# A transformer block on one core: the MLP gate computed on VectorE during fc1, `rows` of three vectors, and the last store issued without other stores' waits

## The chip, the cores and the metric

The kernel runs on one core of a Trainium2 chip. A core has a matrix engine (TensorE, "PE" in the profile; its weight loads are listed as "PEld"), a vector engine (VectorE, "DVE"), a scalar engine (ScalarE, "ACT"), a general engine (GpSimd, "POOL"), a sync engine that issues most transfers (SyncE, "SP"), and 16 DMA engines that all queues share. Operands lie in SBUF, an on-chip memory of 128 partitions; matmul results lie in PSUM, eight banks of 512 f32 values per partition. The engines run their own instruction lists and wait for one another by semaphores. The metric is the device time of one execution in microseconds (us), smaller is better.

## The reference

One block of a diffusion transformer, two samples of 256 tokens, width D = 1152, two heads, MLP width 4608, all in bf16:

```python
mod = (_silu(c) @ w_mod).reshape(B, 6, 1, D)
shift_a, scale_a, gate_a, shift_m, scale_m, gate_m = [mod[:, i] for i in range(6)]
h = _layernorm(x) * (1 + scale_a) + shift_a
q, k, v = split(h @ wqkv)
a = attention(q, k, v) @ wo
x = x + gate_a * a
h2 = _layernorm(x) * (1 + scale_m) + shift_m
m = _gelu(h2 @ w_fc1) @ w_fc2
return x + gate_m * m
```

The condition `c` has one row per sample; each of the six modulation vectors has 1152 values per sample. The change concerns how the last one, `gate_m` (the "MLP gate"), is computed. Its only use is the product with the result of fc2, at the very end.

## The kernel before, in words

All of SBUF is one tensor, `arena`, and all of PSUM one tensor, `psum`; every buffer is a slice at a fixed offset, and several buffers share an offset one after another. Therefore the profile names only `arena` and `psum`, and steps are told apart by source lines.

The program is recorded as units of work, each with an engine, a modelled duration and its reads and writes. `Sched.schedule` orders the units: TensorE's and SP's lists stay in the order of the source, the other engines take the ready unit with the longest modelled path behind it. `Sched.emit` turns dependences into semaphore waits. TensorE's records all carry line 681 (matmul) or 684 (transposition), those of transfers line 662.

The stages in TensorE's order, with the names used later:

1. `silu(c)` becomes a 128x18 tile `ST` (nine chunks of 128 values for two samples). The scale vectors of the attention, the normalization of `x`, then the projections of K and Q; `sh`, the shift vector, by `quad_mm`: four matmuls at a time, each of two rows (the samples) on its own 32-partition quadrant of the array (line 895 transposes its result).
2. Scores, softmax, the value projection `v_proj`, and between two of its parts `rows`.
3. `pv` (probabilities times values), the output projection `wo_tile` with the gated residual (line 1034 multiplies by the attention gate `GA` on VectorE, line 1035 adds `x` on POOL), the second normalization, and `xn2_T`, which transposes on TensorE and applies scale and shift of the MLP on VectorE (1053) and ScalarE (1056) into `H2T`.
4. fc1: 36 tiles of 128 MLP columns. The first eight run for 256 tokens at a time, the others for 512; ScalarE applies Gelu (1066) and writes `GT[f]`.
5. fc2: for each of four token tiles three pieces of 384 columns (the last piece of the last tile is cut into 224, 96 and 64 columns after its first 384-column pieces). VectorE multiplies by the MLP gate `GM` (1145) and adds the residual (1146), SP stores.

`rows` multiplies `ST` by `WMODR`, four of the six column blocks of `w_mod`: attention gate, MLP shift, MLP scale, MLP gate. For each of nine contraction chunks it fills three PSUM banks with four quadrants of 384 columns each, 108 matmuls. ScalarE copies the two gates to `ROWS` (676), VectorE transposes shift and scale into per-partition form (976). POOL then issues four small stores of the gates to a scratch tensor in DRAM and four loads that broadcast them to all 128 partitions (`GA`, and `gate_load(1, GM)` for the MLP gate).

SP issues the transfers strictly in order, and a wait of one holds up those behind it. Behind the weights of attention come `ld_modr` (`WMODR`), `ld_wo`, the first four fc1 weight blocks, three quarters of the fc2 weights `WFC2`, its last quarter, the other five fc1 blocks, and the output stores. `WFC2` lies on the place that `WMODR` has before. Ahead of the last store, SP waits until all stores but the last two have landed (lines 469 to 471); at the end of the program it waits for the last two (485, 486).

Of the kernel before, what the change touches and what calls it, by code (L numbers as in the profile page):

```python
# [171 lines left out]
class Sched:  # L172
# [225 lines left out]
    def emit(self, nc, block, sems, dma_sems):  # L398
        order = self.order
        eidx = {e: 0 for e in ENGINES}  # L400
        dma_cnt = [0] * len(dma_sems)
        n_other = getattr(self, "n_other_dma_sems", 8)
        n_sp = len(dma_sems) - n_other
        di = 0
        dj = 0
        for e in ENGINES:
            for u in order[e]:
                for ins in u.instrs:
                    if u.dma_bytes > 0:
                        if e == "sp":  # L410
                            k = di % n_sp
                            di += 1
                        else:
                            k = n_sp + dj % n_other
                            dj += 1
                        dma_cnt[k] += 16
                        ins.dma_sem = k
                        ins.dma_val = dma_cnt[k]
                    else:
                        eidx[e] += 1  # L420
                        ins.eidx = eidx[e]
        self.final_counts = dict(eidx)
        self.final_dma = list(dma_cnt)
        snap = {}
        stats = {"waits": 0}

        def sem_of(d):
            if d.dma_sem is not None:
                return ("d", d.dma_sem), d.dma_val
            return ("e", d.unit.eng), d.eidx  # L430

        allu = sorted(self.units, key=lambda u: (u.start, u.uid))
        known = {e: {} for e in ENGINES}
        waits = {}
        for u in allu:
            e = u.eng
            kn = known[e]
            for ins in u.instrs:
                need = {}
                for d in ins.deps:  # L440
                    k, v = sem_of(d)
                    if need.get(k, 0) < v:
                        need[k] = v
                wl = []
                for k, v in sorted(need.items(), key=lambda kv: (-kv[1], str(kv[0]))):
                    if kn.get(k, 0) >= v:
                        continue
                    wl.append((k, v))
                    kn[k] = v
                    for d in ins.deps:  # L450
                        if sem_of(d) == (k, v):
                            sn = snap.get(d.gidx)
                            if sn:
                                for kk, vv in sn.items():
                                    if kn.get(kk, 0) < vv:
                                        kn[kk] = vv
                            break
                waits[ins.gidx] = wl
                stats["waits"] += len(wl)
                snap[ins.gidx] = dict(kn)  # L460
        self.wait_stats = stats

        outs = [ins for u in order["sp"] for ins in u.instrs if ins.is_out]
        last_out = outs[-1]

        def run_engine(e, eng_handle):
            for u in order[e]:
                for ins in u.instrs:
                    if ins is last_out:
                        for o in outs[:-2]:  # L470
                            eng_handle.wait_ge(dma_sems[o.dma_sem], o.dma_val)
                    for (k, v) in waits[ins.gidx]:
                        if k[0] == "d":
                            eng_handle.wait_ge(dma_sems[k[1]], v)
                        else:
                            eng_handle.wait_ge(sems[k[1]], v)
                    bi = ins.fn(eng_handle)
                    if ins.dma_sem is not None:
                        bi.then_inc(dma_sems[ins.dma_sem], 16)
                    else:  # L480
                        bi.then_inc(sems[e], 1)
            if e == "sp":
                for o in outs[-2:-1]:
                    eng_handle.wait_ge(dma_sems[o.dma_sem], o.dma_val)
                eng_handle.wait_ge(dma_sems[last_out.dma_sem], last_out.dma_val)

        block.sync(lambda eng: run_engine("sp", eng))
        block.tensor(lambda eng: run_engine("pe", eng))
        block.scalar(lambda eng: run_engine("act", eng))
        block.vector(lambda eng: run_engine("dve", eng))  # L490
        block.gpsimd(lambda eng: run_engine("pool", eng))
# [4 lines left out]
F32 = mybir.dt.float32  # L496
ALU = mybir.AluOpType
# [47 lines left out]
def build_kernel(nc, x, c, wqkv, wo, w_mod, w_fc1, w_fc2, out):  # L545
# [5 lines left out]
    with (  # L551
# [44 lines left out]
        WO = wmat(O_B, D)  # L596
        WSH = wmat(O_C, D)
        WV = wmat(O_C, D)
        WMODR = wmat(O_R, 4 * D)
        WFC2 = sb(O_R, 4 * W1).rearrange("p (k f) -> p k f", k=JT)  # L600
        WFC1 = [wmat(o, 512) for o in (O_A, O_A + 9216, O_C, O_C + 9216)]
        X = sb(O_X, 9216).rearrange("p (t d) -> p t d", t=4)
# [11 lines left out]
        GA = [sb(O_GA + b * 2304, 2304) for b in range(2)]  # L614
        GM = [sb(o + 18432, 2304) for o in (O_A, O_C)]
        XN2 = [sb(O_R + 4 * W1 - (i + 1) * 2304, 2304) for i in range(4)]
        ROWS = sb(O_R + 4 * W1 - 5 * 2304, 2304)[:, 0:576].rearrange("p (g n) -> p g n", g=2)
        T1 = [sb(O_X + i * 1536, 1536, F32) for i in range(3)]
        OST = [sb(O_X + 4608 + i * 768, 768) for i in range(3)]
        gt_offs = ([O_P + i * 1024 for i in range(8)] + [O_B + i * 1024 for i in range(20)]  # L620
# [8 lines left out]
        HC = sb(misc(72), 72, F32)  # L629
        ST = sb(misc(36), 36)  # L630
        SHA = sb(misc(1152), 1152, F32)
        SC1A = sb(misc(72), 72, F32)
        MT = sb(misc(2304), 2304, F32)
        SHM = MT[:, 0:288]
# [82 lines left out]
        act(200, lambda e: e.activation(out=TH, in_=CT_PS, func=ACTF.Tanh, scale=0.5), [CT_PS], [TH], "c_tanh")  # L717
        dve(170, lambda e: e.tensor_scalar(out=HC, in0=CT_PS, scalar1=0.5, scalar2=None, op0=ALU.mult), [CT_PS], [HC], "c_half")
        dve(170, lambda e: e.scalar_tensor_tensor(out=ST, in0=TH, scalar=1.0, in1=HC, op0=ALU.add, op1=ALU.mult), [TH, HC], [ST], "c_silu")


        def ln_stats_dve(src, chunks, bn_t, mv_t, rstd_t, tag):
# [167 lines left out]
            quad_mm(0, WSH[:, kt, :], 0, 9, kt)  # L890
        dma(WV, wqkv_v[:, :, 2 * D:3 * D], D * D * 2, "ld_wv", run=2304)
        for k0 in range(0, KT, 3):
            dma(WMODR[:, k0:k0 + 3, :], wmod_v[:, k0:k0 + 3, 2 * D:6 * D], 3 * P * 4 * D * 2, "ld_modr%d" % k0)
        MT1 = ps32(0, 0, 288)
        dve(c_dve_psum32(288), lambda e: e.transpose(SHA, MT1), [MT1], [SHA], "sha")  # L895
        for kt in range(KT):
# [66 lines left out]
            copy_on("act" if v_rr[0] % 2 else "dve", V[:, t, ci * CH:(ci + 1) * CH], o, CH, False, "v_ev%d_%d" % (t, ci))  # L963


        row_banks = (3, 4, 5)

        def rows():
            S.unit("pe", KT * 3 * c_mm(CH) + 200.0, "rows")
            for kt in range(KT):  # L970
                for r in range(3):
                    quad_mm(row_banks[r], WMODR[:, kt, :], 12 * r, 12 * r + 12, kt)
            copy_on("act", ROWS[:, 0, :], ps32(3, 0, 288), 288, False, "rows_ev0")
            for i, (bank, c0, n, d0) in enumerate(((3, 288, 96, 0), (4, 0, 384, 96), (5, 0, 96, 480))):
                src, dst = ps32(bank, c0, n), MT[:, d0:d0 + n]
                dve(c_dve_psum32(n), lambda e, src=src, dst=dst: e.transpose(dst, src), [src], [dst], "mt_%d" % i)
            sc, so = MT[:, 288:576].rearrange("p (k r) -> p k r", r=32)[:, :, 0:2], SC1M.rearrange("p (k b) -> p k b", b=2)
            dve(170, lambda e: e.tensor_scalar(out=so, in0=sc, scalar1=1.0, scalar2=None, op0=ALU.add), [sc], [so], "sc1m")
            copy_on("act", ROWS[:, 1, :], ps32(5, 96, 288), 288, False, "rows_ev1")
            for gi in range(2):  # L980
                for b in range(2):
                    dma(scratch[gi, b].rearrange("(k q c) -> q k c", q=4, c=32), ROWS[b:128:32, gi, :].rearrange("p (k c) -> p k c", c=32),
                        2304, "st_g%d%d" % (gi, b), eng="pool")
                if gi == 0:
                    gate_load(0, GA)

        def gate_load(gi, G):
            for b in range(2):
                dma(G[b], scratch[gi, b].partition_broadcast(P), P * D * 2, "ld_g%d%d" % (gi, b), eng="pool")


        PVB = [(0, 1, 2, 6, 7), (3, 4, 5, 0, 1)]
# [29 lines left out]
        def wo_tile(t, before={}):  # L1022
# [16 lines left out]
            dve(170, lambda e: e.scalar_tensor_tensor(out=nm, in0=m, scalar=-1.0, in1=rs, op0=ALU.mult, op1=ALU.mult), [m, rs], [nm], "nmr2_%d" % t)  # L1039
            act(1344, lambda e: e.activation(out=xn2, in_=x1, func=ACTF.Identity, scale=rs, bias=nm), [x1, rs, nm], [xn2], "xn2_%d" % t)  # L1040

        def xn2_T(t):
            b = t // 2
            xn2 = XN2[t]
# [4 lines left out]
            for kt in range(KT):  # L1049
                o, dst = slot[kt], H2T[:, kt, t * 128:(t + 1) * 128]  # L1050
                s1, s2 = SC1M[:, kt * 2 + b:kt * 2 + b + 1], SHM[:, kt * 32 + b:kt * 32 + b + 1]
                if kt < (4 if t < 2 else 6):
                    dve(335, lambda e, o=o, dst=dst, s1=s1, s2=s2: e.tensor_scalar(out=dst, in0=o, scalar1=s1, scalar2=s2, op0=ALU.mult, op1=ALU.add),  # L1053
                        [o, s1, s2], [dst], "h2T_%d_%d" % (t, kt))
                else:
                    act(440, lambda e, o=o, dst=dst, s1=s1, s2=s2: e.activation(out=dst, in_=o, func=ACTF.Identity, scale=s1, bias=s2),  # L1056
# [42 lines left out]
        v_proj(3, 0)  # L1099
        v_proj(3, 1)  # L1100
        v_proj(3, 2)
        gate_load(1, GM)
        wfc1_load(2)
        wfc1_load(3)
        for q4 in range(3):
            dma(WFC2[:, 9 * q4:9 * q4 + 9, :], wfc2_v[:, 9 * q4:9 * q4 + 9, :], 9 * P * D * 2, "ld_wfc2_%d" % q4, run=2304)
        for b in range(2):
            for h in range(2):
# [12 lines left out]
        for f in range(F0 - 2, F0):  # L1121
            fc1_tile(f, 0, 256)
        dma(WFC2[:, 27:36, :], wfc2_v[:, 27:36, :], 9 * P * D * 2, "ld_wfc2_3", run=2304)
        for f in range(F0):
            fc1_tile(f, 256, 256)
        for f in range(F0, JT):
            if f % 4 == 0 and f // 4 >= 4:
                wfc1_load(f // 4)
            fc1_tile(f, 0, 512)

        oi = 0
        for t in range(4):
# [70 lines left out]
```

## Time and profile before

| | |
|---|---|
| median of three runs | 248.95 us (248.63 to 249.59) |
| the profiled execution | 249.1 us, span in the profile 247.1 us |
| granted TensorE clock, mean | 0.996 |
| TensorE (PE) busy | 240.4 us, 97% |
| VectorE (DVE) busy | 69.9 us, 28% |
| ScalarE (ACT) busy | 64.0 us, 26% |
| POOL busy | 21.1 us, 9% |
| DMA | 51.59 MB, 27708 packets |

The span is the profile's own window; the execution's time also holds what lies around it. The page gives busy shares per engine and in 40 slices of the span (each 6.18 us), the chain of work that ended last (followed back from the last instruction to what released it), and groups of instructions with the idle time ahead of them. In a timeline the columns are start, duration, engine, line, operation and operands with their count, and in brackets the idle time before it and what ended that. Idle time of an engine that nobody waits for costs nothing.

### The profile page before, as it was taken

Reading aid. Unit: us, or ns where it says so; the run is one execution under the profiler, and the core shown is the slowest. Engines: PE = TensorE matmul, PEld = TensorE weight load, DVE = VectorE, ACT = ScalarE, POOL = GpSimd, SP = SyncE. Lnnn points to the kernel's source line nnn. Section 1 sums busy time; section 2 is a strip of 40 time slices with the busy share of each in tenths; the row PEclk is TensorE's granted clock in tenths of the full one; section 3 lists DMA queues with packets and bytes.
Section 4 is the critical chain, followed back from the end, with each engine's and each line's share of the span. In section 5 each row is a group of like instructions: output and inputs, shape, how many; then the busy total and the mean of one; then the engine's idle time right before and its main releaser. Section 6 shows DMA issues by size and latency. Waiting matters only on the chain.

```text
span 247.1 us, 4020 instructions
## 1 busy us (share of the span) xinstructions
PE 240.4 (97%) x1757; PEld 148.0 (60%) x1767; DVE 69.9 (28%) x179; ACT 64.0 (26%) x130; POOL 21.1 (9%) x35
## 2 busy tenths in 40 slices
PE   7999999999999999999999999999999999999993
PEld 2589844566656766798544444444666666666683
DVE  3742440546222779850000000000022111111122
ACT  5630340344312306983323332223000000000000
POOL 1300000000034175600000000000000000000000
PEclk9999999999999999999999999999999999999998
DMA  7999999999999999999953450000000000000000
GB/s 242 360 376 392 391 369 412 422 428 423 400 382 323 327 369 391 390 376 397 352 159 102 170 191 0 0 3 0 0 19 16 16 16 30 20 16 19 16 16 20
DMA packets 27708, 51.59 MB, mean 209 GB/s; under 512 B 1563, under 2 KB 15659, under 8 KB 26539
## 3 DMA queue, kind: packets, MB, share of 16 engines
q1 hardware_dynamic: 27216, 50.14, 56.1%
q0 software_dynamic: 448, 1.19, 1.5%
q8 instruction: 14, 0.23, 0.4%
q14 instruction: 3, 0.02, 0.0%
q10 hardware_dynamic: 27, 0.00, 0.0%
HBM read 50.14 MB, written 1.19 MB: 208 GB/s over the span
## 4 chain that ended last, share of the span: by engine, by line
PE 92%; DMA 3%; ACT 1%; SPq 1%; issue 0%; DVE 0%
PE psum L681 91%; DMA arena<-in_w_mod_dram 3%; PE psum L684 2%; ACT arena L1056 1%; SPq L662 1%; ACT arena L1040 1%; DVE arena L786 0%; DVE arena L1145 0%; DVE arena L1146 0%; DVE arena L777 0%
## 5 line engine op out<-in xcount | busy, mean ns | idle before, releaser
L681 PE MATMUL psum<-arena 128*128 128x384 bf16 (+8 forms) x1668 | 237.0, 312 | 2.4 <-POOL arena L704 1.4
L681 PEld LDWEIGHTS psum<-arena 128*128 128x128 bf16 (+1 forms) x1678 | 142.5, 97 | 92.2 <-issue 3.6
L1145 DVE TENSOR_TENSOR arena<-psum,arena 128x384 f32<-128x384 f32 (+3 forms) x14 | 7.0, 500 | 119.2 <-PE psum L681 119.2
L1066 ACT ACTIVATE arena<-psum 128x512 bf16<-128x512 f32 (+1 forms) x44 | 22.5, 522 | 42.6 <-PE psum L681 42.6
L676 ACT ACTIVATE arena<-psum 128x512 bf16<-128x512 f32 (+7 forms) x30 | 15.7, 546 | 35.7 <-PE psum L681 33.3
L678 DVE CAST arena<-psum 128x512 bf16<-128x512 f32 (+3 forms) x21 | 13.0, 627 | 26.4 <-PE psum L681 26.3
L1035 POOL TENSOR_TENSOR arena<-arena 128x384 f32<-128x384 f32 x12 | 10.9, 911 | 10.5 <-DVE arena L1034 9.3
L725 DVE BATCH_NORM_STATS2 arena<-arena 128x6 f32<-128x384 f32 (+1 forms) x18 | 9.5, 549 | 1.1 <-DMA arena<-in_x_dram 1.0
L1040 ACT ACTIVATE arena<-arena 128x1152 bf16<-128x1152 f32 x4 | 5.4, 1352 | 9.5 <-DVE arena L1039 9.5
L662 POOL DMA_DIRECT2D dit_scratch<-arena x4 | 2.7, 669 | 60.3 <-ACT arena L676 60.3
L684 PEld LDWEIGHTS psum<-arena 128*128 128x128 bf16 (+1 forms) x89 | 5.9, 98 | 2.7 <-DMA arena<-in_c_dram 0.8
L684 PE MATMUL psum<-arena 128*128 128x128 bf16 (+1 forms) x89 | 7.3, 219 | 0.2
L1034 DVE TENSOR_TENSOR arena<-psum,arena 128x384 f32<-128x384 f32 x12 | 6.6, 548 | 3.2 <-PE psum L681 2.6
L1146 DVE TENSOR_TENSOR arena<-arena 128x384 bf16<-128x384 f32 (+3 forms) x14 | 7.0, 501 | 0.5
L1056 ACT ACTIVATE arena<-psum,arena 128x128 bf16<-128x128 bf16 x16 | 6.1, 460 | 3.2 <-PE psum L684 2.5
L1053 DVE TENSOR_SCALAR arena<-psum,arena 128x128 bf16<-128x128 bf16 x20 | 5.5, 336 | 2.0 <-PE psum L684 1.8
L938 ACT ACTIVATE arena<-psum,arena 128x256 bf16<-128x256 f32 x8 | 3.7, 470 | 6.9 <-PE psum L681 5.4
L729 POOL TENSOR_TENSOR arena<-arena 128x1 f32<-128x1 f32 x6 | 3.3, 551 | 8.3 <-DVE arena L728 8.3
L901 ACT ACTIVATE arena<-arena 128x256 bf16<-128x256 bf16 x6 | 2.5, 495 | 3.3 <-DVE arena L895 3.3
L934 DVE TENSOR_REDUCE arena<-psum 128x2 f32<-128x512 f32 x4 | 2.8, 690 | 1.5 <-PE psum L681 1.5
L786 DVE TENSOR_SCALAR arena<-psum,arena 128x256 bf16<-128x256 bf16 x7 | 2.4, 349 | 2.7 <-PE psum L684 1.4
L942 DVE TENSOR_TENSOR arena<-arena 128x512 bf16<-128x512 bf16 x4 | 2.7, 687 | 0.1
(37 smaller groups left out, 32.0 us busy)
## 6 DMA issues: line engine op xcount, KB each, us to landing
arena<-in_w_mod_dram SPq DMA_DIRECT2D x3, 3456.0 KB, 26.5
arena<-in_w_fc_dram SPq DMA_DIRECT2D x9, 1152.0 KB, 8.8
arena<-in_w_fc_dram SPq DMA_DIRECT2D x4, 2592.0 KB, 20.9
arena<-in_wqkv_dram SPq DMA_DIRECT2D x18, 288.0 KB, 10.0
arena<-in_w_mod_dram SPq DMA_DIRECT2D x3, 864.0 KB, 12.5
arena<-in_wqkv_dram SPq DMA_DIRECT2D x1, 2592.0 KB, 10.9
arena<-in_wo_dram SPq DMA_DIRECT2D x1, 2592.0 KB, 39.0
arena<-in_w_mod_dram SPq DMA_DIRECT2D x3, 480.0 KB, 7.3
```

The lines of the kernel that those rows point to most:

```text
L676: act(c_act(n), lambda e: e.activation(out=dst, in_=src, func=ACTF.Copy), [src], [dst], name)
L678: dve(c_dve_psum16(n) if psum16 else c_dve_psum32(n), lambda e: e.tensor_copy(dst, src), [src], [dst], name)
L681: S.instr(lambda e: e.matmul(o, lhsT=l, rhs=r, start=st, stop=sp, **kw), reads=[l, r], writes=[o])
L684: S.instr(lambda e: e.transpose(o, i_, idn), reads=[i_, idn], writes=[o])
L725: dve(550, lambda e, s=s, o=o: e.bn_stats(out=o, in_=s), [s], [o], "bn_%s_%d" % (tag, ci))
L1034: dve(550, lambda e, o=o, ga=ga, x1c=x1c: e.tensor_tensor(out=x1c, in0=o, in1=ga, op=ALU.mult), [o, ga], [x1c], "wo_t1_%d_%d" % (t, ci))
L1035: S.op("pool", 930, lambda e, xs=xs, x1c=x1c: e.tensor_tensor(out=x1c, in0=x1c, in1=xs, op=ALU.add), reads=[x1c, xs], writes=[x1c], name=" ...
L1040: act(1344, lambda e: e.activation(out=xn2, in_=x1, func=ACTF.Identity, scale=rs, bias=nm), [x1, rs, nm], [xn2], "xn2_%d" % t)
L1056: act(440, lambda e, o=o, dst=dst, s1=s1, s2=s2: e.activation(out=dst, in_=o, func=ACTF.Identity, scale=s1, bias=s2), [o, s1, s2], [dst], ...
L1066: act(c_act(ntok), lambda e: e.activation(out=dst, in_=o, func=ACTF.Gelu_apprx_tanh), [o], [dst], "gelu_%d_%d" % (f, tok0))
L1145: dve(c_dve_psum32(w), lambda e, o=o, gm=gm, t1=t1: e.tensor_tensor(out=t1, in0=o, in1=gm, op=ALU.mult), [o, gm], [t1], "fc2_t1_%d_%d" % ( ...
L1146: dve(c_dve_32(w), lambda e, t1=t1, x1c=x1c, ost=ost: e.tensor_tensor(out=ost, in0=t1, in1=x1c, op=ALU.add), [t1, x1c], [ost], "fc2_out_%d ...
```

## The change

- `rows` computes three vectors (attention gate, MLP shift, MLP scale): two PSUM banks with 14 and 13 groups of 32 columns in four quadrants, that is 448 and 416 columns, 72 matmuls. `WMODR` holds three column blocks. One eviction on ScalarE instead of two, two transpositions on VectorE (416 and 160 columns) instead of three, two small stores and two broadcast loads on POOL instead of four and four.
- The MLP gate's column block of `w_mod`, `WGM`, is loaded by itself behind the first four fc1 blocks, into the place of the first quarter of `WFC2`.
- `mlp_gate` runs on VectorE, ordered behind the last VectorE evacuation of `xn2_T(3)`: for each sample nine products of a weight chunk (128 contraction rows by 1152 columns) with a per-partition scalar of `silu(c)`, accumulated in f32 in `ACC2`. The sum over the 128 partitions: a 32x32 block transposition of the 2304 columns, a sum over groups of 32, three moves between quadrants of partitions and three additions, a conversion to bf16, and a small transposition. POOL stores the result to the scratch tensor in two pieces and loads it back as a broadcast. `ST32`, an f32 copy of `ST`, is made on POOL.
- The first quarter of `WFC2` is loaded behind the last fc1 block, once the products have read `WGM`. The buffer into which the 2304 columns are transposed lies on the place of `GT[28]` to `GT[35]`, so the Gelu of tile 28 waits for the sum over groups.
- The last store is issued as soon as its data is ready. The waits for all other stores stand behind it, at the end of the program.

```diff
-                    if ins is last_out:
-                        for o in outs[:-2]:
-                            eng_handle.wait_ge(dma_sems[o.dma_sem], o.dma_val)
...
             if e == "sp":
-                for o in outs[-2:-1]:
+                for o in outs[:-1]:
                     eng_handle.wait_ge(dma_sems[o.dma_sem], o.dma_val)
...
-        WMODR = wmat(O_R, 4 * D)
+        WMODR = wmat(O_R + W1, 3 * D)
+        WGM = wmat(O_R, D)
+        ACC2 = sb(O_X, 9216, F32)
+        ACC = ACC2.rearrange("p (b d) -> p b d", b=2)
+        ACT = sb(O_HX, 9216, F32)
...
+        pool(200, lambda e: e.tensor_copy(ST32, ST), [ST], [ST32], "c_silu32")
...
-            dma(WMODR[:, k0:k0 + 3, :], wmod_v[:, k0:k0 + 3, 2 * D:6 * D], 3 * P * 4 * D * 2, "ld_modr%d" % k0)
+            dma(WMODR[:, k0:k0 + 3, :], wmod_v[:, k0:k0 + 3, 2 * D:5 * D], 3 * P * 3 * D * 2, "ld_modr%d" % k0)
...
-        row_banks = (3, 4, 5)
+        row_parts = ((3, 0, 14), (4, 14, 27))
 
         def rows():
...
             for kt in range(KT):
-                for r in range(3):
-                    quad_mm(row_banks[r], WMODR[:, kt, :], 12 * r, 12 * r + 12, kt)
-            copy_on("act", ROWS[:, 0, :], ps32(3, 0, 288), 288, False, "rows_ev0")
-            for i, (bank, c0, n, d0) in enumerate(((3, 288, 96, 0), (4, 0, 384, 96), (5, 0, 96, 480))):
+                for bank, g0, g1 in row_parts:
+                    quad_mm(bank, WMODR[:, kt, :], g0, g1, kt)
+            copy_on("act", ROWS, ps32(3, 0, 288), 288, False, "rows_ev")
+            for i, (bank, c0, n, d0) in enumerate(((3, 288, 160, 0), (4, 0, 416, 160))):
...
+        def mlp_gate(prev):
+            for b in range(2):
+                for kt in range(KT):
+                    o, w, s1 = ACC[:, b, :], WGM[:, kt, :], ST32[:, b * 9 + kt:b * 9 + kt + 1]
+                    if kt == 0:
+                        u = dve(1300, lambda e, o=o, w=w, s1=s1: e.tensor_scalar(out=o, in0=w, scalar1=s1, scalar2=None, op0=ALU.mult),
+                                [w, s1], [o], "gm_%d_%d" % (b, kt))
+                    else:
+                        u = dve(1300, lambda e, o=o, w=w, s1=s1: e.scalar_tensor_tensor(out=o, in0=w, scalar=s1, in1=o, op0=ALU.mult, op1=ALU.add),
+                                [w, s1, o], [o], "gm_%d_%d" % (b, kt))
+                    S.order_after(u, prev)
+            pool(100, lambda e: e.memset(GB, 0.0), [], [GB], "gb0")
+            dve(2600, lambda e: e.transpose(ACT, ACC2), [ACC2], [ACT], "gm_T")
+            t3 = ACT.rearrange("p (g r) -> p g r", r=32)
+            dve(2600, lambda e: e.tensor_reduce(out=GP[:, 0, :], in_=t3, axis=AX.X, op=ALU.add), [t3], [GP[:, 0, :]], "gm_red")
+            for q in range(1, 4):
+                i_, o_ = GP[32 * q:32 * q + 32, 0, :], GP[0:32, q, :]
+                dve(200, lambda e, i_=i_, o_=o_: e.tensor_copy(o_, i_), [i_], [o_], "gm_mv%d" % q)
+            for a_, b_ in ((0, 1), (2, 3), (0, 2)):
...
+            dve(200, lambda e: e.tensor_copy(gb, g0), [g0], [gb], "gm_bf")
+            dve(200, lambda e: e.transpose(GT2, GB), [GB], [GT2], "gm_T2")
+            lin = scratch[1].rearrange("b (g c) -> (b g) c", c=32)
+            dma(lin[0:64].rearrange("(j p) c -> p j c", j=2), GT2[:, 0:64].rearrange("p (j c) -> p j c", j=2), 4096, "st_gm0", eng="pool")
+            dma(lin[64:72], GT2[0:8, 64:96], 512, "st_gm1", eng="pool")
+            for b in range(2):
+                dma(GM[b], scratch[1, b].partition_broadcast(P), P * D * 2, "ld_gm%d" % b, eng="pool")
...
-        gate_load(1, GM)
         wfc1_load(2)
         wfc1_load(3)
-        for q4 in range(3):
+        dma(WGM, wmod_v[:, :, 5 * D:6 * D], D * D * 2, "ld_gm", run=2304)
+        for q4 in range(1, 3):
             dma(WFC2[:, 9 * q4:9 * q4 + 9, :], wfc2_v[:, 9 * q4:9 * q4 + 9, :], 9 * P * D * 2, "ld_wfc2_%d" % q4, run=2304)
...
         dma(WFC2[:, 27:36, :], wfc2_v[:, 27:36, :], 9 * P * D * 2, "ld_wfc2_3", run=2304)
+        mlp_gate(last_h2T[0])
         for f in range(F0):
...
+        dma(WFC2[:, 0:9, :], wfc2_v[:, 0:9, :], 9 * P * D * 2, "ld_wfc2_0", run=2304)
```

More of the change, by code (lines that the diff above doesn't have):

```diff
@@ L616, in build_kernel @@
         XN2 = [sb(O_R + 4 * W1 - (i + 1) * 2304, 2304) for i in range(4)]
-        ROWS = sb(O_R + 4 * W1 - 5 * 2304, 2304)[:, 0:576].rearrange("p (g n) -> p g n", g=2)
+        ROWS = sb(O_R + 4 * W1 - 5 * 2304, 2304)[:, 0:288]
         T1 = [sb(O_X + i * 1536, 1536, F32) for i in range(3)]
@@ L631, in build_kernel @@
         SHA = sb(misc(1152), 1152, F32)
+        ST32 = sb(misc(72), 72, F32)
+        GP = sb(O_GA, 1152, F32).rearrange("p (q g) -> p q g", q=4)
+        GB = sb(O_GA + 1152, 192)[0:32, :]
+        GT2 = sb(O_GA + 1344, 192)[0:32, :]
         SC1A = sb(misc(72), 72, F32)
@@ L963, in v_proj @@
             copy_on("act" if v_rr[0] % 2 else "dve", V[:, t, ci * CH:(ci + 1) * CH], o, CH, False, "v_ev%d_%d" % (t, ci))
-        row_banks = (3, 4, 5)
+        row_parts = ((3, 0, 14), (4, 14, 27))
         def rows():
-            S.unit("pe", KT * 3 * c_mm(CH) + 200.0, "rows")
+            S.unit("pe", KT * 864 / 2.4 + 500.0, "rows")
             for kt in range(KT):
-                for r in range(3):
-                    quad_mm(row_banks[r], WMODR[:, kt, :], 12 * r, 12 * r + 12, kt)
-            copy_on("act", ROWS[:, 0, :], ps32(3, 0, 288), 288, False, "rows_ev0")
-            for i, (bank, c0, n, d0) in enumerate(((3, 288, 96, 0), (4, 0, 384, 96), (5, 0, 96, 480))):
+                for bank, g0, g1 in row_parts:
+                    quad_mm(bank, WMODR[:, kt, :], g0, g1, kt)
+            copy_on("act", ROWS, ps32(3, 0, 288), 288, False, "rows_ev")
+            for i, (bank, c0, n, d0) in enumerate(((3, 288, 160, 0), (4, 0, 416, 160))):
                 src, dst = ps32(bank, c0, n), MT[:, d0:d0 + n]
@@ L978, in rows @@
             dve(170, lambda e: e.tensor_scalar(out=so, in0=sc, scalar1=1.0, scalar2=None, op0=ALU.add), [sc], [so], "sc1m")
[L979 to L985, printed above, removed]
@@ L987, in gate_load @@
-        def gate_load(gi, G):
-            for b in range(2):
-                dma(G[b], scratch[gi, b].partition_broadcast(P), P * D * 2, "ld_g%d%d" % (gi, b), eng="pool")
+            for b in range(2):
+                dma(scratch[0, b].rearrange("(k q c) -> q k c", q=4, c=32), ROWS[b:128:32, :].rearrange("p (k c) -> p k c", c=32),
+                    2304, "st_g%d" % b, eng="pool")
+            for b in range(2):
+                dma(GA[b], scratch[0, b].partition_broadcast(P), P * D * 2, "ld_g%d" % b, eng="pool")
@@ new lines, in mlp_gate @@
+        def mlp_gate(prev):
[17 more added lines that the diff above has]
+            for a_, b_ in ((0, 1), (2, 3), (0, 2)):
+                x_, y_ = GP[0:32, a_, :], GP[0:32, b_, :]
+                dve(200, lambda e, x_=x_, y_=y_: e.tensor_tensor(out=x_, in0=x_, in1=y_, op=ALU.add), [x_, y_], [x_], "gm_add%d" % b_)
+            g0, gb, gt = GP[0:32, 0, :], GB[0:32, 0:72], GT2
+            dve(200, lambda e: e.tensor_copy(gb, g0), [g0], [gb], "gm_bf")
[3 more added lines that the diff above has]
+            dma(lin[64:72], GT2[0:8, 64:96], 512, "st_gm1", eng="pool")
+            for b in range(2):
+                dma(GM[b], scratch[1, b].partition_broadcast(P), P * D * 2, "ld_gm%d" % b, eng="pool")
@@ L1040, in wo_tile @@
             act(1344, lambda e: e.activation(out=xn2, in_=x1, func=ACTF.Identity, scale=rs, bias=nm), [x1, rs, nm], [xn2], "xn2_%d" % t)
+        last_h2T = [None]
         def xn2_T(t):
@@ L1052, in xn2_T @@
                 if kt < (4 if t < 2 else 6):
-                    dve(335, lambda e, o=o, dst=dst, s1=s1, s2=s2: e.tensor_scalar(out=dst, in0=o, scalar1=s1, scalar2=s2, op0=ALU.mult, op1=ALU.add),
+                    last_h2T[0] = dve(335, lambda e, o=o, dst=dst, s1=s1, s2=s2: e.tensor_scalar(out=dst, in0=o, scalar1=s1, scalar2=s2, op0=ALU.mult, op1=ALU.add),
                         [o, s1, s2], [dst], "h2T_%d_%d" % (t, kt))
```

## The prediction

> **What bounds the kernel now.** I read the page first, then the chain of waits, then two stretches of the timeline and the issue rows of the stores.
>
> ```profile
> PE 240.4 (97%) x1757; PEld 148.0 (60%) x1767; DVE 69.9 (28%) x179; ACT 64.0 (26%) x130; POOL 21.1 (9%) x35
> DVE  3742440546222779850000000000022111111122
> ...
> q8 instruction: 14, 0.23, 0.4%
> ```
>
> TensorE works in 97% of the span. VectorE (DVE) does nothing in eleven slices of 6.18 us, about 110 to 178 us; this is where the change puts its new work. The chain that ended last:
>
> ```profile
> 64.92 30.90 PE psum L681 x283
> ...
> 172.28 70.95 PE psum L681 x505
> 243.24 0.02 issue
> 243.26 0.24 DVE arena L1145
> 243.50 0.02 issue
> 243.52 0.23 DVE arena L1146
> ```
>
> From 64.92 us on it is nearly all TensorE, save one excursion over ScalarE at 96 us. So only two things shorten the run: fewer TensorE microseconds, or a shorter tail behind the last matmul at 243.24. An operation on another engine is free until somebody on this chain waits for it. The timeline around `rows` (the small matmuls of the modulation vectors):
>
> ```profile
> 66.31 4.16 PEld L681 LDWEIGHTS psum<-arena 128*2 128x2 bf16 x108 [0.32 <-issue]
> ...
> 70.80 5.15 PEld L681 LDWEIGHTS psum<-arena 128*128 128x128 bf16 x33 [0.33 <-issue]
> 71.00 0.73 ACT L676 ACTIVATE arena<-psum 128x288 bf16<-128x288 f32 x2 [4.09 <-PE psum L681]
> 71.00 0.91 DVE L976 STREAM_TRANSPOSE arena<-psum 128x96 f32<-128x96 f32 x3 [5.71 <-PE psum L681]
> ```
>
> The first load of the 108 stands at 66.31, the next unit's at 70.80: `rows` holds TensorE for 4.49 us. The last three stores, in the timeline of SyncE's queue (SPq), and who SP waited for:
>
> ```profile
> 241.35 0.33 SPq L662 DMA_DIRECT2D out_dram<-arena  x1
> ...
> 242.61 0.33 SPq L662 DMA_DIRECT2D out_dram<-arena  x1
> ...
> 245.28 0.33 SPq L662 DMA_DIRECT2D out_dram<-arena  x1
> ```
>
> ```profile
> SPq L471 <- DMA out_dram<-arena: 1.9, 1, 1.9
> SPq L485 <- DMA out_dram<-arena: 1.1, 1, 1.1
> ```
>
> ```profile
> out_dram<-arena SPq DMA_DIRECT2D x11, 96.0 KB, 1.6
> out_dram<-arena SPq DMA_DIRECT2D x1, 56.0 KB, 3.8
> out_dram<-arena SPq DMA_DIRECT2D x1, 24.0 KB, 2.7
> out_dram<-arena SPq DMA_DIRECT2D x1, 16.0 KB, 1.4
> ```
>
> The last result is ready at 243.52 + 0.23 = 243.75, but its store is issued at 245.28, because SP waits at L471 until the 56 KB store has landed (241.35 + 3.8 = 245.15). Every other one of eleven larger stores lands in 1.6 us. It lands at 246.7, and the span ends at 247.1.
>
> **Part 1, three vectors instead of four in `rows`.** Nine contraction tiles times three banks times four quadrants of 384 columns (108 matmuls) become nine times two banks times four of 448 or 416 (72). A group of four takes 4.49 / 27 = 166 ns at 384 columns. The same kind of group for the shift vector, 288 columns, takes (31.29 - 30.08) / 9 = 134 ns, from the starts of its weight loads. So a group costs by its columns: 0.33 ns a column between these rows. At the mean of 432 columns that is 182 ns, times 18 = 3.28 us, a gain of 1.21; in proportion to the columns alone it is 4.49 x 0.75 = 3.37, a gain of 1.12. Counting by weight loads (36 x 41.6 ns) would give 1.50, which the shorter 288-column groups speak against, since they have as many loads a group and cost less. I take 1.15, ends 1.1 and 1.5. No wait can take it back: the units behind it use other PSUM banks and loaded operands, and the chain shows no stall of TensorE before 96 us.
>
> **Part 2, what else moves around `rows`.** One ScalarE eviction of 288 columns (half of the 0.73) goes; the three transposes of 0.91 us in all become two over the same 576 columns, the second behind ScalarE's eviction of the same bank. Two stores and two loads of the gate leave POOL's queue (0.67 and 0.57 us each), so the attention gate arrives earlier than now, when the first product of the output projection waits 0.6 us for it. That wait is not on the chain: VectorE has caught up with TensorE by 91.47. A conversion of 18 columns on POOL falls into its idle time between 1.4 and 6.5 us, a clear of a 32x96 tile into a gap of 0.56 us between two additions. All of it: nothing.
>
> **Part 3, the new VectorE chain.** It starts behind the last VectorE eviction of the fourth token tile, 108.49 + 1.60 = 110.1. Eighteen products over 1152 columns: no such instruction is in the trace. The nearest rows are tensor-tensor operations of line 1146, 558 ns at 384 columns and 225 at 64, so 1.04 ns a column plus 0.16 us, and 1.36 us at 1152. With 0.03 between them: 18 x 1.39 = 25.0, to 135.1. Below it stands the 16-bit tensor-scalar operation of 1152 columns at 0.574 us, above it I set twice the row, 2.7. A 2304-column transpose by the transposes of 96 and 384 columns (263 and 543 ns) takes 2.4 us, the sum over 32 by the reduction of 512 columns (690 ns) and the same slope 2.6: 140.1. Three moves, three additions, a conversion and a small transpose at 0.2 us: 141.7. Then two stores and two loads on POOL, which is empty from 104.85: two issues, 5.4 us to landing, two issues, 9.6: about 159.
>
> Who waits for it? First, the Gelu of fc1 tile 28, whose output takes the buffer that the summed product is read from: it stands at 120.25 + 20 x 1.945 = 159.15, against 140.1. Behind it on ScalarE stand the last seven Gelus, and through their banks TensorE. Second, the fc2 weights' first quarter, which now waits on SP for the last of the 18 products (135.1). SP issues the last fc1 weights at 141.98 anyhow, so this wait is over when SP comes to it. Behind it in SP's queue stand only the output stores, the first at 179.73. With the 20.9 us of the 2592 KB rows it lands at 163, needed at 172.28. Third, the MLP gate itself, 159 against VectorE's first fc2 product at 178.55. The load of the gate's weights takes the place in the queue that the first quarter has now (issued 85.30, plus 20.9 is 106.2, against 110.1), with 2.6 MB less ahead of it; being some us late would cost VectorE alone. So nothing is added to the chain, with covers of 19, 9 and 19 us.
>
> **Part 4, the last store.** Without the waits it is issued at 243.75 + 0.03 = 243.78, 1.50 us earlier. Thirteen waits move behind it; a satisfied one costs SP no more than the 0.03 us from a VectorE end to an issue, 0.4 in all, inside the store's flight. What the flight will be is the open cost. Its own row says 1.4 (gain 1.5), the 24 KB one before it 2.7 (gain 0.2), the 56 KB one 3.8 (loss 0.9).
>
> Why were these two slow? Windows that begin ever later show one q8 packet (16 KB, 1.6 us on one of 16 DMA engines) starting at 242.45, and at 244.25 all but 14 packets of the two stores gone; so one engine's share was held up behind it. The q8 packets of the fc2 stage start at 185.2, 206.4, 226.6 and 242.5, with 127 matmuls in the last full interval: I infer that they are TensorE's instructions, one for some 256. The change takes 36 matmuls and 36 loads out ahead of it, so that packet comes 72 instructions later in the program, at 34 ns a matmul in the last piece 1.2 us later: 243.7 to 245.3 on the old clock. The new last store's packets would go at 244.5 (0.75 after the issue, as now). One engine's nine would wait for 245.3 and land by about 246.0, since the 56 KB store landed 1.1 us after the packet's end with 18 packets to send. If the packet falls behind the program's end, there is no delay. I take a flight of 2.05 us, midway between its own row and the 24 KB row that suffered the same: landing at 245.83, a gain of 0.85, and keep 1.4 and 3.8 for the range.
>
> The Trainium skill, "Runtime: NRT & Kernel Launch", Instruction fetch mechanics, says that instructions are refilled in blocks of 256 and that crossing a block is mostly hidden; by that the tail would gain the whole 1.5 and the time would be that of the first rival. The trace agrees on the spacing, and shows the hiding fail at the end, where two stores of 56 and 24 KB took 3.8 and 2.7 us. The skill's "DMA: Bandwidth & Descriptors", Queues, rings and completion order, says that a completion lands only after the earlier writes of its DMA engine; by that the last store can't be reported before the 24 KB one, at 245.3 in this trace, and the gain would stop at 1.4.
>
> **Sum.** The profiled execution took 249.1, its span 247.1; 2.0 lie outside. 249.1 - 1.15 - 0.85 = 247.1. The median is 0.15 below that execution, so 246.95.
>
> **Rivals.** *The store flies undisturbed*: 248.95 - 1.15 - 1.5 = 246.3. For it: 1.4 and eleven times 1.6; against: the 72 instructions are too close to the distance. *The store is disturbed in full, as the 56 KB one was*: 248.95 - 1.15 + 0.9 = 248.7, no change; the same would show if the rows gained nothing. Against it: the packet would have to start just as the store's do. *The VectorE chain is too long* (slower): the fc2 weights wait for the eighteenth product. With 10.9 us to landing (the 2592 KB load of wqkv) they come at 110.1 + 18c + 10.9, later than 172.28 from c = 2.85 us a product. From c = 3.03 the loss of 3.3 us outweighs the gain by 0.5%. At c = 3.3 fc2 starts 8.1 late: 248.95 - 2.0 + 8.1 = 255. For it: the product with an f32 accumulator has no row. Against it: the rows of f32 operations agree on about 1.04 ns a column, and this is 2.4 times it.
>
> **Chances.** Forecast 0.48 (246.6 to 247.5), undisturbed store 0.27 (246.0 to 246.6), no change 0.14, long chain 0.11. About 0.5%, 1.25 us, is what a measurement of this kernel tells from no change. Faster 0.75, same 0.14, slower 0.11. The range 246.1 to 248.3 leaves out the long chain and part of the no-change case.
>
> **What would show it.** `rows` of 3.3 to 3.4 us between the first small weight load and the next large one, all later TensorE work earlier by that; VectorE busy for about 31 us from 109 us with products of 1.36 us, and fc1 and fc2 without new idle time on TensorE; the last store issued 0.03 us behind VectorE's last end, landing after 1.4 to 2.7. I am wrong if the products take over 2.8 us, if TensorE waits at the border of fc1 and fc2, or if the three last stores now delay each other.

## The result, and the profile after

The changed kernel takes 246.83 us (median of four, 246.34 to 247.31) against 249.0 us for the kernel before (now four executions, 248.63 to 249.59): a ratio of 0.9916, 95% interval 0.9887 to 0.9945. Forecast were 246.95 and a range of 246.1 to 248.3. The profiled execution took 246.34 us with a span of 244.6 us; 1.74 us lie outside. The page:

```profile
span 244.6 us, 3987 instructions
...
PE 239.6 (98%) x1731; PEld 147.0 (60%) x1731; DVE 99.3 (41%) x206; ACT 63.7 (26%) x129; POOL 21.4 (9%) x37
...
DVE  3743350555322779869999600000012222111112
...
q8 instruction: 13, 0.21, 0.4%
```

VectorE's slices 19 to 23, empty before, are now filled; TensorE has 36 matmuls and their loads less (1731 weight loads, from 1767; the trace of the kernel before lacks the records of ten matmuls); and there are 13 q8 packets where there were 14. The chain that ended last:

```profile
107.42 134.79 PE psum L686 x846
242.21 0.02 issue
242.24 0.24 DVE arena L1180
242.47 0.02 issue
242.50 0.23 DVE arena L1181
```

TensorE runs from 107.42 to 242.21 without a break in the chain, so none of the new waits is on it. The last matmul ends 1.03 us earlier than before (243.24). Behind it the span lasts 2.4 us, where it lasted 3.9. The timeline around `rows`:

```profile
66.39 3.02 PEld L686 LDWEIGHTS psum<-arena 128*2 128x2 bf16 x72 [0.32 <-issue]
...
69.78 4.18 PEld L686 LDWEIGHTS psum<-arena 128*128 128x128 bf16 x27 [0.37 <-issue]
69.98 0.41 ACT L681 ACTIVATE arena<-psum 128x288 bf16<-128x288 f32 x1 [2.99 <-PE psum L686]
```

From 66.39 to 69.78 are 3.39 us, against 4.49. The new VectorE chain, in its timeline:

```profile
108.99 1.54 DVE L996 TENSOR_SCALAR arena<-arena 128x1152 f32<-128x1152 bf16 x2
110.44 21.35 DVE L999 SCALAR_TENSOR_TENSOR arena<-arena 128x1152 f32<-128x1152 bf16 x16
131.82 2.58 DVE L1003 STREAM_TRANSPOSE arena<-arena 128x2304 f32<-128x2304 f32 x1
134.44 2.55 DVE L1005 TENSOR_REDUCE arena<-arena 128x72 f32<-128x2304 f32 x1
...
138.55 0.27 DVE L1014 STREAM_TRANSPOSE arena<-arena 32x96 bf16<-32x96 bf16 x1
```

The products follow one another at 21.35 / 16 = 1.33 us, and the chain lasts 29.8 us, to 138.82. The issue rows of the stores, with KB each and us to landing:

```profile
out_dram<-arena SPq DMA_DIRECT2D x11, 96.0 KB, 1.6
out_dram<-arena SPq DMA_DIRECT2D x1, 56.0 KB, 1.5
...
out_dram<-arena SPq DMA_DIRECT2D x1, 24.0 KB, 1.5
...
out_dram<-arena SPq DMA_DIRECT2D x1, 16.0 KB, 1.4
```

The last store is issued at 242.75, 0.02 behind VectorE's last end, and all three narrow stores land like the wide ones. The 3.8 and 2.7 us are gone. The last q8 packet starts at 231.5, eleven microseconds ahead of the last matmul's end; in the kernel before it started at 242.47 and lasted 1.6 us, while the first two of the three narrow stores were in flight.

So two things happened together at the end: the waits ahead of the last store went, and so did the q8 packet that had fallen on those stores, which the prediction took for a packet of TensorE's instructions. The tail's gain has two possible owners, and the first four runs below separate them.

### The profile page after: what moved, and what is told of

It reads as the page before. It is cut to its first block, busy times and chain, and to the rows that moved or that the text cites. A ratio compares the mean times of both kernels' runs of the same rounds, so it can differ in the third digit from the quotient of the medians.

```text
span 244.6 us, 3987 instructions
## 1 busy us (share of the span) xinstructions
PE 239.6 (98%) x1731; PEld 147.0 (60%) x1731; DVE 99.3 (41%) x206; ACT 63.7 (26%) x129; POOL 21.4 (9%) x37
## 4 chain that ended last, share of the span: by engine, by line
PE 93%; DMA 3%; ACT 1%; SPq 1%; DVE 0%; issue 0%
PE psum L686 91%; DMA arena<-in_w_mod_dram 3%; PE psum L689 2%; ACT arena L1088 1%; SPq L667 1%; ACT arena L1070 1%; DVE arena L792 0%; DVE arena L1180 0%; DVE arena L1181 0%; DVE arena L783 0%
## 5 line engine op out<-in xcount | busy, mean ns | idle before, releaser
L686 PE MATMUL psum<-arena 128*128 128x384 bf16 (+9 forms) x1642 | 236.1, 312 | 1.8 <-POOL arena L709 1.4
L999 DVE SCALAR_TENSOR_TENSOR arena<-arena 128x1152 f32<-128x1152 bf16 x16 | 21.3, 1409 | 0.0
```

Source lines behind the costliest of these rows:

```text
L686: S.instr(lambda e: e.matmul(o, lhsT=l, rhs=r, start=st, stop=sp, **kw), reads=[l, r], writes=[o])
L999: u = dve(1300, lambda e, o=o, w=w, s1=s1: e.scalar_tensor_tensor(out=o, in0=w, scalar=s1, in1=o, op0=ALU.mult, op1=ALU.add), [w, s1, o], ...
```

## The experiments

### Who shortened the tail

Four kernels were timed beside each other on one chip, where the kernel before took 248.51 us (17 executions, 247.95 to 249.33). First the changed kernel again.

> The changed kernel once more, to have it timed beside the experiments. My account of its 2.5 us shorter span: 1.1 from the rows stage and 1.5 from the tail behind the last matmul, of which the tail part came because one 16 KB packet of TensorE's instructions (q8) no longer falls on the last stores. Expected: 246.3 to 247.3, a profile without a q8 packet after 238 us, the last three stores landing in 1.4 to 1.6 us. If the tail gain were a matter of the removed waits alone, the same times would come out; the next three runs tell the two apart.

Measured: 246.52 us (246.34 to 247.03), ratio 0.9922 (0.9906 to 0.9938). The stores landed in 1.5, 1.5 and 1.4 us, and no q8 packet came behind 231.9.

Next, the old waits put back:

```diff
+                    if ins is last_out:
+                        for o in outs[:-2]:
+                            eng_handle.wait_ge(dma_sems[o.dma_sem], o.dma_val)
...
-                for o in outs[:-1]:
+                for o in outs[-2:-1]:
```

> The changed kernel with the old waits of SP ahead of the last store put back; rows and the VectorE chain stay. Theory of the instruction packet: the 56 KB store is issued at 240.3 and lands after 1.5 us at 241.8, so the waits are over before the last data is ready at 242.7; the last store is issued within 0.1 us of that, and the time equals that of the changed kernel within 0.3 us (246.5 to 247.2). Rival, the waits themselves cost the time: the last store is issued 1.5 us later and the time is 248.1 to 248.6.

Measured: 246.72 us (246.48 to 247.03), ratio 0.9926 (0.9911 to 0.9942), not distinguishable from the changed kernel. Who SP waited for, and the last store in SP's timeline:

```profile
SPq L485 <- DMA out_dram<-arena: 1.1, 1, 1.1
SPq L476 <- DVE arena L1184: 0.5, 1, 0.5
```

```profile
242.81 0.33 SPq L670 DMA_DIRECT2D out_dram<-arena  x1
```

Ahead of the last store SP now waits for VectorE (L1184 is the residual addition), no longer for a store. The data is ready at 242.49 + 0.23 = 242.72 and the issue stands at 242.81: twelve waits on stores that have long landed cost under 0.1 us. The rival, 248.1 to 248.6, has fallen: in a kernel in which no packet meets the stores, these waits cost nothing that the times resolve.

The opposite, the kernel before with only the waits moved behind the last store (the first two pieces of the diff alone):

> The kernel before with only the last store's waits moved behind it. Both theories expect the last store 0.03 us behind VectorE's last end, 1.5 us earlier than before. Instruction packet: it still starts about 0.8 us ahead of the last matmul's end and still holds up the 56 and the 24 KB store (2.5 to 3.8 us); the last store's packets come after its end, so it lands in 1.4 to 2.0 us, and the gain is 0.9 to 1.5 us: 247.5 to 248.1. Waits alone: 1.5 us, 247.4. If the stores slow each other: no gain, 248.7 or more.

Measured: 247.73 us (247.34 to 248.06), ratio 0.9968 (0.9957 to 0.9978): a gain of 0.78 us by the medians. The time lies in the expected range; the gain is just below the 0.9 to 1.5 expected, because the kernel before takes 248.51 on this chip and not 249.0. The profile's span is 245.6, and the tail behind the last matmul 2.4 us. Issue rows:

```profile
q8 instruction: 14, 0.23, 0.4%
...
out_dram<-arena SPq DMA_DIRECT2D x1, 56.0 KB, 3.0
out_dram<-arena SPq DMA_DIRECT2D x1, 24.0 KB, 1.9
...
out_dram<-arena SPq DMA_DIRECT2D x1, 16.0 KB, 1.4
```

The packet is still there, starting at 242.3 and lasting 1.1 us, and the two stores are still slow; but the last one no longer waits for them (issued 243.77, data ready 243.74), and its own packets start behind the q8 packet's end. So that edit does gain by itself, as a way round the packet.

Then the kernel before with the packet moved and everything else kept. Waits that have long been met are put ahead of 184 matmuls of fc1; a pair of them makes one instruction:

```diff
+                    if e == "pe" and pad[0] and u.name.startswith("fc1_") and u.name.endswith("_0") and int(u.name.split("_")[1]) >= F0:
+                        pad[0] -= 1
+                        eng_handle.wait_ge(sems["act"], 1)
+                        eng_handle.wait_ge(sems["act"], 1)
```

> The kernel before, with 184 further instructions in TensorE's list, semaphore waits that have long been met, one ahead of each of 184 matmuls of fc1. With 256 instructions a packet this moves the packets as taking 72 out does. Nothing else is changed: rows of four vectors, all old waits. Instruction packet: no q8 packet after 240 us, the last stores land in 1.4 to 1.6 us, SP's wait ahead of the last store is gone, and the kernel gains 1.3 to 1.6 us: 247.4 to 247.7, if the waits themselves stay hidden behind matmuls of 216 ns (fc1 lengthened by less than 0.2 us). Rival, the waits cost the time: last store at 245.3 as before, no gain, 248.7 to 249.2.

Measured: 247.58 us (247.31 to 247.83), ratio 0.9962 (0.9947 to 0.9977): a gain of 0.93 us from 184 instructions more. The time lies in the expected range, but the expected gain, 1.3 to 1.6, was missed between the medians; the profile's span, 245.5, is 1.6 below the 247.1 of the kernel before. Issue rows, and the last part of the chain:

```profile
out_dram<-arena SPq DMA_DIRECT2D x1, 56.0 KB, 1.7
out_dram<-arena SPq DMA_DIRECT2D x1, 24.0 KB, 1.5
...
out_dram<-arena SPq DMA_DIRECT2D x1, 16.0 KB, 1.4
```

```profile
108.27 134.79 PE psum L687 x846
243.06 0.02 issue
243.08 0.24 DVE arena L1151
```

The same 134.79 us from 108.27 to the end of fc2 as in the changed kernel says that the added waits cost TensorE nothing. The last q8 packet starts at 232.3, 10.8 us ahead of the last matmul's end; in the changed kernel the last one starts 10.7 us ahead of it. So 184 instructions more and 72 fewer put the packets at the same distance from the end, as they must if a packet holds 256. With the old waits in place the last store is issued at 243.66, 0.09 behind its data, and the tail is 2.4 us. In this run a q14 packet remains near the end (241.5), as in the kernel before (241.6); the stores are fast all the same, so q14 was not the cause.

Why 0.93 and not 1.6? The kernel before does not always lose as much as its profile shows. Its 17 executions on this chip have spans from 246.0 to 247.3, with a median of 246.5; the profiled one, at 247.1, was taken in the first comparison and would lie in the upper part here. The slowed stores landed in 3.8 and 2.7 us in the profile of the kernel before, where the packet took 1.6 us, and in 3.0 and 1.9 with the last store alone moved, where it took 1.1. I put the spread down to how long the packet takes and how it meets the stores; that was not shown execution by execution.

The wide stores bear the theory out, though nobody waits for them. In the kernel before, the one issued at 226.53 met the thirteenth q8 packet (226.6 to 227.8) and landed in 2.4 us instead of 1.6; nine of its 144 packets, one sixteenth, started only after the q8 packet's end. In the run with 20 added instructions described below, one issued at 208.06 met a q8 packet and landed in 3.4. That the stores and the q8 packet share one of the 16 DMA engines is inferred from such counts; no record names the engine.

### The packet brought back, and its edge

On a second chip (kernel before 248.48 us, 11 executions, 248.14 to 249.44) the changed kernel got 36, and then 20, further TensorE instructions in the same way. The changed kernel itself was not timed on this chip.

> The changed kernel with 36 further TensorE instructions (met semaphore waits ahead of 36 matmuls of fc1). By the count of 256 a packet, the next q8 packet then comes again before the end, half as far from it as in the kernel before: it should start about at the last matmul's end (from 0.3 us before to 0.5 after) and last 1.6 us. Instruction packet: it falls on the 24 KB store and on the last one; these land 2 to 3.5 us after their issue, and the time is 0.2 to 1.0 us above the changed kernel's: 247.0 to 247.8. If the place of the packet is of no account: the changed kernel's time, 246.3 to 247.3, with stores of 1.4 to 1.6 us.

Measured: 246.91 us (246.71 to 247.19), ratio 0.9928 (0.9909 to 0.9947). That is just below the 247.0 to 247.8 expected, and inside the 246.3 to 247.3 of the other theory: the time does not decide between them. The profile does:

```profile
q8 instruction: 14, 0.23, 0.4%
...
out_dram<-arena SPq DMA_DIRECT2D x1, 56.0 KB, 1.5
...
out_dram<-arena SPq DMA_DIRECT2D x1, 24.0 KB, 2.6
...
out_dram<-arena SPq DMA_DIRECT2D x1, 16.0 KB, 1.9
```

The fourteenth packet is back. It starts at 242.06, 0.17 us ahead of the last matmul's end, inside the forecast of -0.3 to +0.5, and it now falls on the last two stores instead of the first two of the three: the 24 KB store took 2.6 us, the last one 1.9, a little under the 2 to 3.5 expected. The packet lasted 1.1 us, not 1.6. The span is 245.1 and the tail 2.9 us.

> The same with 20 further instructions: the packet, if it comes at all, comes still later, 0.1 to 0.8 us behind the last matmul's end, and falls on the last store's own packets. Instruction packet: either 0.5 to 1.2 us above the changed kernel (the last store landing in 2 to 3 us), or no packet and no loss, where TensorE's list ends ahead of the place. No account: no loss.

Measured: 246.71 us (246.36 to 247.21), ratio 0.9921 (0.9902 to 0.994). Thirteen packets, stores of 1.5, 1.5 and 1.4 us, tail 2.4 us. Between 20 and 36 instructions more, then, the packet enters the run. In the profiles it costs 0.5 us of tail there; the times, 0.2 us apart with overlapping spreads, do not resolve it.

### How much room the VectorE chain has

Each product is made two or three times, the later sums overwriting the earlier:

```diff
-            for b in range(2):
+            for b in [i // 2 for i in range(4)]:
                 for kt in range(KT):
```

> The changed kernel with each of the 18 products made twice (the first sum is overwritten by the second). The products took 22.8 us in the changed kernel, so they end at 109.0 + 45.7 = 154.7. By my covers the first quarter of the fc2 weights then lands at 161 to 166, needed at 171.3; the Gelu of tile 28 waits until the sum at 159.8, 1.7 us late, which its spare PSUM banks absorb; the MLP gate arrives at about 170, needed at 177.5. Expected: the changed kernel's time within 0.3 us. If one of the covers is thinner than I worked out, TensorE shows idle time at the end of fc1 and the time rises by it.

Measured on the second chip: 246.91 us (246.78 to 247.11), ratio 0.9929 (0.9908 to 0.995). The changed kernel had 0.9922 on the other chip, so by the ratios there is no loss. In its timeline:

```profile
157.42 2.55 DVE L1005 TENSOR_REDUCE arena<-arena 128x72 f32<-128x2304 f32 x1
...
160.07 1.08 ACT L1098 ACTIVATE arena<-psum 128x512 bf16<-128x512 f32 x2 [3.08 <-PE psum L686]
```

The Gelu of tile 28 starts right behind the reduction instead of at 158.3, and the next one directly behind it; the chain shows no new wait of TensorE (the last matmul ends at 242.47). The banks took up the delay, as worked out. The first quarter of the fc2 weights lands at 154.80 + 9.0 = 163.8, inside the 161 to 166 expected.

> The changed kernel with each product made three times: they end at 109.0 + 68.5 = 177.5, past the start of fc2 at 171.3. The sum is ready at 182.6, so the Gelu of tile 28 and, through the banks, fc1's tile 34 wait for it: fc1 ends at about 187. The fc2 weights land at 184 to 188. Expected: fc2 starts at 187 to 188.5, 16 to 17.5 us late, time 262.5 to 264.5. If the wait of the weights alone counted, 184 at the earliest, 13 us late, 259.5.

Measured, one execution: 264.72 us, span 262.6. The chain:

```profile
155.91 21.27 DVE arena L999 x16
177.19 0.02 issue
177.21 2.59 DVE arena L1003
179.80 0.02 issue
179.82 2.56 DVE arena L1005
...
182.47 0.61 ACT arena L1098
183.08 0.05 issue
183.12 6.06 PE psum L686 x16
189.18 0.05 issue
189.23 70.95 PE psum L686 x505
```

Here VectorE bounds the run: the sum at 182.4 releases the Gelu of tile 28, that releases a bank, and TensorE goes on at 183.12 after 15.4 us of idleness. fc2 starts at 189.23, a little behind the forecast of 187 to 188.5, and the time is 0.2 above its range: the last 16 matmuls of fc1, of 512 columns, took 6.06 us, 379 ns each instead of 216 (a tile of nine takes 1.945 us). The windows show a lower clock there (columns: stretch, its length, busy time of each engine, granted clock, DMA share, GB/s):

```profile
183.10:184.00 0.90, 0.88 (x3) 0.33 (x4) 0.80 (x5) 0.90 (x3) 0.00 (x0) 0.50 1.06 412
...
187.00:188.00 1.00, 1.00 (x4) 0.39 (x3) 0.00 (x0) 0.60 (x1) 0.88 (x2) 0.50 0.06 16
...
189.30:192.00 2.70, 2.70 (x17) 1.60 (x17) 0.00 (x0) 0.60 (x1) 0.00 (x0) 1.00 0.32 123
```

After the pause the granted clock was 0.50, until about 188 us. It was the wait for the Gelu's buffer, not that for the fc2 weights, that ended last: the weights landed at 177.20 + 9.1 = 186.3, 2.9 us before fc2 started.

## Why the prediction was right, and where its working was not

**`rows`**: 1.15 us forecast, 1.10 by the starts of the weight loads, the lower end of 1.1 to 1.5, and 1.03 by the last matmul's end, just below it. A group of 432 columns took 3.39 / 18 = 188 ns, not the 182 that the line between 288 and 384 columns gave; proportion to the columns (187) was right.

**The moves around `rows`** cost nothing, as said: the excursion over ScalarE at 96 us is still in the chain with the same lengths (1.16, 1.29 and 0.70 us).

**The VectorE chain**: 1.39 us a product from start to start (1.36 and 0.03 between them), 1.33 measured; 2.4 and 2.6 us for transposition and reduction, 2.58 and 2.55 measured; 31.6 us in all, 29.8 measured. The first product of each sample, without an addition, took 0.81 us, between the two bounds set for a product. Nobody waited. That the chain can last 22.8 us longer at no cost is shown by the doubled products, and that a wait stands behind it by the tripled ones. The rival of a chain that is too long is right that the run can be bound this way, but not in the path it named: with three times the products fc2 was held up through the Gelu of tile 28 and not through the fc2 weights.

**The last store** is the term that was mis-sized. I took a flight of 2.05 us, with the instruction packet falling on it; it was 1.4. The step that failed is the placing of the packet: moved by 72 instructions, I put it at 243.7 to 245.3 on the old clock. It did not come at all; only with 36 of the 72 put back did it, 20 were too few. The working turned 72 instructions into 1.2 us and did not ask whether the list still had them. Between the packet's start at 242.47 and the end, the trace of the kernel before shows 20 matmuls and 16 weight loads, 36 instructions; the profile with the last store alone moved shows 26 and 22 behind its packet. A shift of 72, or of 52, goes past that end, one of 36 does not, and this is what the three runs found. It is a reading after the fact. The prediction had named the case ("if the packet falls behind the program's end") and given it the smaller chance. Two smaller slips beside it: twelve waits moved behind the last store, not thirteen, and not every wide store of the kernel before landed in 1.6 us, which is the median of the eleven; the one that met a packet took 2.4.

So the mechanism that ran is that of the undisturbed rival, and that the median, 246.83, lies nearer to the forecast of 246.95 than to the rival's 246.3 is luck. A second mis-sizing pulls the other way: the sum took the whole tail of one execution of the kernel before, whose span of 247.1 lies near the top of what the 17 later executions show. Removing the packet is worth 1.6 us between spans of profiles and 0.93 between medians. With 1.03 from `rows` that makes 1.03 + 0.93 = 2.0, as much as the 1.15 + 0.85 of the forecast; the medians differ by 2.2 in the first comparison and 2.0 in the second. That the profiled execution took 246.34, the rival's figure, is luck as well: only 1.74 us of it lie outside the span, and another execution with the same span, 244.6, took 246.6.

**What the packet is**: the inference that q8 carries TensorE's instructions, about 256 to a packet, is borne out by the changed kernel and by those with added TensorE instructions, whose packets moved as their TensorE lists did. Between its last four packets the changed kernel has 128 to 131 matmuls and 127 to 130 weight loads each time. One thing stays open: in the kernel before 158 and 157 lie between the last two, and no run shows why that interval is longer. The Trainium skill's "Runtime: NRT & Kernel Launch", Instruction fetch mechanics, gives the 256 and says that crossing a block is mostly hidden. For TensorE the traces agree: its 134.79 us of fc1 and fc2 have no break at the packets that fall into them. They do not show it hidden for stores under way, which land later, and it cost time where SP waited for one.

**The credit of the edits** differs from the prediction's account. It gave the tail's gain to the removed waits. The runs give it to the packet's absence, which is a by-product of part 1; in the changed kernel the removed waits are worth nothing that was measured (246.72 against 246.52), while in the kernel before they are worth 0.78. The two do not add up: either alone brings the tail of the profile from 3.9 to 2.4 us.

## What to carry to other kernels

Where one engine is busy for 97% of the run, work moved from it to an idle engine is worth its time on the first one, as long as every buffer it holds and every transfer it delays is released early enough; write down each such cover in microseconds, and doubling the moved work shows in one run whether it holds. Before a wait at the end is blamed for its length, look at why the thing waited for is late: here an identical edit was worth 0.78 us in one kernel and nothing that was measured in another. And state a gain against the spread of the kernel before, not against the one execution that was profiled.

## What the runs showed of the hardware

- A packet of instructions (16 KB, 0.9 to 1.6 us in these traces) delays stores that it meets: the 24 and 56 KB stores landed in 1.9 to 3.8 us instead of 1.5 to 1.7, and wide ones in 2.4 and 3.4 instead of 1.6. Where SP waited for one of them at the end, that cost the kernel 0.8 to 0.9 us of 248.5 between medians. The packet's place depends on the number of instructions in the list, so 184 useless instructions made the kernel faster (0.93 us).
- Satisfied semaphore waits, one instruction ahead of each of 184 matmuls of 216 ns, cost TensorE nothing measurable (134.79 us with and without); twelve on SP cost less than 0.1 us.
- After 15.4 us without matmuls the granted TensorE clock was 0.50 for some 5 us, with 379 ns for a matmul of 512 columns instead of 216 (one execution).
- On VectorE a product of 1152 bf16 values with a per-partition scalar, added to an f32 accumulator, takes 1.33 us from start to start (1.41 each by its record), and the same product without the addition 0.73 (0.81 by its record).
